# Attention and mixture of experts in one kernel: masks that read rows from partition 0, reversed keys for heads 4 to 7, and a later expert table

## The chip, the cores and the metric

The kernel runs on one core of a Trainium2 chip. The metric is the device time of one execution in microseconds (us). Five engines work beside each other, each through its own queue in order: PE (TensorE, matmuls and transposes), DVE (VectorE), ACT (ScalarE), POOL (GpSimd) and SP, which here only issues DMAs. POOL also issues the DMAs that scatter rows by an index. An engine's next instruction waits in its queue until the semaphores that it names have been raised, and what stands behind it waits too.

## The reference, cut to what matters

```python
# attention: q, k, v are (8, 8, 576, 64); ALiBi bias; a query sees itself and the 127 keys before it
scores = scale * (q @ k.T) + slopes[h] * -(pos_q - pos_k)
scores = where((rel >= 0) & (rel < 128), scores, -1e9)
attn = exp(scores - max); attn /= sum + 1e-9
x = (attn @ v) laid out as 4608 tokens of 512 values
# mixture of 8 experts, top 1
logits = (x / |x|) @ (expert_emb / |expert_emb|).T / tau
e = argmax(logits); gate = softmax(logits)[e]
out[token] = gate * (relu(x @ w1[e]) @ w2[e])
```

## The kernel before, in words

**Stages.** Attention comes first, up to about 243 us of the trace. The three large groups of tokens are routed to experts while it still runs, and the rows of each token are scattered to `xs`, a DRAM table sorted by expert. Then the largest expert's first 384 rows (the head) and all experts are multiplied. PE ends the program's chain in that second part.

**Tiles.** There are 36 attention tiles T: four pairs of batches times nine blocks of 64 queries (n = 0 to 8). A tile has two halves hf, of four heads each: hf 0 is heads 0 to 3, hf 1 heads 4 to 7. Partitions 0 to 63 of a score bank hold the queries of one batch, 64 to 127 those of the other. A half-tile takes this path: scores on PE into two PSUM banks (L588 adds the bias, L596 the products); with n > 1 a merge on DVE (L606) lays the far block of keys, of which only a triangle counts, into the masked triangle of the own block, so that 128 columns hold 192 keys; a maximum on DVE (L611); exponentials on ACT (L619); a transposition on PE (L627) after which keys lie on partitions; a copy to SBUF on ACT (L634, the tile `pq`); the mask on POOL (L647); the products with the values on PE (L658 for `pq`, L668 for the corners in `mb`); division on DVE (L682, L687); and the split of x into two fp16 parts (L703 on DVE, L714 on POOL), which L718 transposes by DMA for the logits (L724, L728).

**The mask.** After the transposition the 64 merged keys of a half-tile lie on partitions 0 to 63 or on 64 to 127: `mixed(T, hf)` is (n + hf) mod 2, and `halves[...]` picks that half of the partitions. Two POOL instructions of 64x512 take the merged block apart: the first writes one triangle to `mb`, the second leaves the other in `pq`. So of each tile's two masks one reads from partition 0 and one from partition 64: for even n it is hf 1 that reads from partition 64, for odd n hf 0. There are 56 masks, of 28 tiles with n > 1.

**Scatters.** `put` (L828, L829) issues one scattering DMA of a tile's 128 rows on POOL. Those of the first group of eight tiles stand among the masks of pair 1, those of the second among the masks of pair 2, and those of the third come in one row near attention's end.

**Order of the work.** The order on each engine is fixed at build time by a planner (`Plan`): each job has an engine, an estimated duration, what it comes after, the buffers that it takes, and a due time; the planner runs them in a model and emits them in that order. The planner's model has no wait of a mask for a scatter. PSUM has eight banks; `start` lets a job take a bank if its ring (`sc` 6 banks, `fl` 2, `ps` 4 for values, logits and the rest) has its oldest holder done, and if enough banks are open. The job `expert0` to `expert14` (L524 to L538) normalise the table of expert embeddings; `EXPERT` is the earliest planned time of them, in ns. The first of them, on DVE, needs the DMA of `tau`, which L492 issues behind two loads of keys, two of queries and the embeddings.

Of the kernel before, what the change touches and what calls it, by code (L numbers as in the profile page):

```python
# [23 lines left out]
P = 128  # L24
# [41 lines left out]
RING = {'sc': 'sc', 'fl': 'fl', 'av': 'ps', 'lg': 'ps', 'misc': 'ps'}  # L66
BANKS = {'sc': 6, 'fl': 2, 'ps': 4}
NBANK = 8
AHEAD = 4
ORDER = -1e9  # L70
KBUFS, QBUFS = 2, 4
VBUFS = 8
XBUFS = 16
# [6 lines left out]
SWITCH = 90  # L80
BOND = 5000
FREE = {"SP": 0, "POOL": 5300, "DVE": 4200, "PE": 3600, "ACT": 2100}
EXPERT = 6000
DUE = {'load': -13.7, 'loadv': -4.0, 'k': -7.0, 'q': -5.8, 'v': 2.0, 'score': 0.0, 'merge': 1.3, 'max': 2.0, 'exp': 3.5, 'flip': 3.8, 'phi': 3.3, 'mask': 5.6, 'av': 6.8, 'norm': 8.6, 'xhi': 7.1, 'xlo': 11.3, 'xnorm': 9.8, 'xdma': 10.5, 'logit': 9.6, 'route': 13.5, 'put': 16.7}


# [5 lines left out]
SHARE = {'x': 1, 'x2': 0.75}  # L92
QENG = ['ACT', 'DVE']
FENG = ['ACT']
PEBUFS, PQBUFS, MBUFS = 3, 4, 2


class Plan:
# [4 lines left out]
        self.yields = 0  # L103
        self.pooled, self.banks, self.given = (), [], []

    def job(self, name, eng, ns, emit, after=(), makes=(), uses=(), due=0.0, fill=False, early=0.0, dma=0, land=None, moves=0, port=False, lock=(), form=None):
        after = [a if isinstance(a, tuple) else (a, 0) for a in after]
        self.jobs[name] = dict(
            name=name, eng=eng, ns=ns, emit=emit, after=after, makes=list(makes), uses=list(uses), due=due, fill=fill, early=early, dma=dma, land=land, moves=moves, port=port, lock=lock, form=form
        )  # L110
# [18 lines left out]
    def run(self, free):  # L129
# [11 lines left out]
        def start(j):  # L141
            e = j["eng"]
            if "can" not in j:
                j["can"] = max([j["early"]] + [self.seen(a, j["name"], end) + extra for a, extra in j["after"]])
            t = max(free.get(e, 0.0), j["can"])
            seen = {}
            for ring, _ in j["makes"]:
                lst = rings.setdefault(ring, [])
                k = len(lst) + seen.get(ring, 0)
                seen[ring] = seen.get(ring, 0) + 1  # L150
                if k >= self.caps[ring]:
                    if k - self.caps[ring] >= len(lst):
                        return None
                    for u in self.users[lst[k - self.caps[ring]]]:
                        if u not in end:
                            return None
                        t = max(t, self.seen(u, j["name"], end))
            n = sum(1 for ring, _ in j["makes"] if ring in self.pooled)
            if n:
                open_ = sorted(opens(j))  # L160
                if len(open_) < n:
                    return None
                t = max(t, open_[n - 1][0])
            if j["port"]:
# [75 lines left out]
def kernel(  # L240
# [54 lines left out]
    nc.scalar.preload_act_table_set("natural_log_exp_and_others")  # L295
    ident = const.tile([P, P], F32, name="ident")
    make_identity(nc, ident)
    identb = const.tile([P, P], BF16, name="identb")
    nc.vector.tensor_copy(identb, ident)
    tab = const.tile([P, HP, 2 * P], BF16, name="tab")  # L300
# [21 lines left out]
    merges = [const.tile([P, 64], I32, name=f"merge_{i}") for i in range(2)]  # L322
# [24 lines left out]
    ones = const.tile([P, P], BF16, name="ones")  # L347
    nc.gpsimd.memset(ones, 1.0)
# [105 lines left out]
    def attention(actx):  # L454
# [114 lines left out]
        def mixed(T, hf):  # L569
            return (tiles[T][1] + hf) % 2  # L570
# [32 lines left out]
        def merge_dve(T, hf, j):  # L603
            ps, x = sc[T, hf, j], mixed(T, hf)
            lo, hi = ps[:, :, 0:64], ps[:, :, P : P + 64]
            nc.vector.copy_predicated(*((hi, lo) if x else (lo, hi))[:1], merges[x].unsqueeze(1).to_broadcast([P, 2, 64]), lo if x else hi)  # L606

        def max_dve(T, hf, j):
            nm_t[T, hf, j] = sm.tile([P, 2], F32, tag="nm", name=f"nm{j}_{T}_{hf}", bufs=8)
# [27 lines left out]
            return FENG[(2 * T + hf) % len(FENG)]  # L637

        def mask_pool(T, hf):
            n = tiles[T][1]  # L640
# [19 lines left out]
        def corners_pe(T):  # L660
            n = tiles[T][1]
            for i in range(4):
                for hf in range(2):
                    r = halves[mixed(T, hf)]
                    x = mb_t[T] if n else pq_t[T, hf]
# [314 lines left out]
        for T in range(NT):  # L980
# [22 lines left out]
            for hf in range(2):  # L1003
# [33 lines left out]
                if n > 1:  # L1037
                    ready = f"mask{u}"
                    J(
                        ready, "POOL", 1188, lock=(590, 590), emit=lambda a=a: mask_pool(*a), after=[f"phi{u}"], makes=[] if hf else [("mb", ("mb", T))],  # L1040
                        uses=[("pq", u), ("mb", T)], due=due("mask", u),
                    )
                J(
                    f"av{u}", "PE", 496 if n else 50, form="columns", emit=lambda a=a: values_pe(*a),
                    after=[ready] + then("put", T - XBUFS) + [f"v_one{x}" for x in vs], makes=[(RING["av"], ("av", u))],
                    uses=[("pq", u), ("av", u)] + [("v", y) for y in vs], due=due("av", u),
                )
            if n != 1:
                J(
                    f"avs{T}", "PE", 456, form="quarters", emit=lambda T=T: corners_pe(T), after=[f"av{u0}", f"av{u0 + 1}"],  # L1050
                    uses=[("av", u0), ("av", u0 + 1)] + ([("mb", T)] if n else [("pq", u0), ("pq", u0 + 1)]) + [("v", y) for y in vs], due=due("av", u0 + 1) + 300,
                )
            for hf in range(2):
                u = u0 + hf
                J(
                    f"recip{u}", "DVE", 95, lambda a=(T, hf): sums_dve(*a), after=[f"av{u}" if n == 1 else f"avs{T}"], makes=[("rs", ("rs", u))],
                    uses=[("av", u)], due=due("norm", u),
                )
                J(
                    f"norm{u}", "DVE", 332, lambda a=(T, hf): normalize(*a), after=[f"recip{u}"],  # L1060
                    makes=[] if hf else [("xf", ("xf", T))], uses=[("av", u), ("rs", u), ("xf", T)], due=due("norm", u) + 300,
                )
            u = u0 + 1
# [970 lines left out]
```

## Time and profile before

| | |
|---|---|
| median of 3 runs | 621.3 us (619.61 to 626.68) |
| the profiled execution | 624.13 us, of which the span from first to last instruction is 622.4 us |
| PE, DVE, ACT, POOL busy | 561.6, 459.8, 342.7, 259.9 us |
| mean granted clock of PE | 0.95 |
| first and last mask | 25.8 us, 239.3 us |
| first matmul of the experts behind the head (L1429) | 279.3 us |

Busy times are sums over stages with different limits; what a wait is worth is read from its own stage. A releaser in brackets is what ended an engine's idle time, by the profile's inference; of a wait for several semaphores it names the one that seems to have come last. Matmul ends are modelled.

### The profile page before, as it was taken

The numbers are of one execution on the slowest core, as the hardware profiler recorded it, in microseconds if no ns is written. First come the engines' busy times: TensorE is split into PE (matmuls) and PEld (weight loads), VectorE is DVE, ScalarE is ACT, GpSimd is POOL, SyncE is SP. The second block draws the span as 40 slices with busy tenths as digits, with TensorE's granted clock in tenths as the row PEclk, the third lists the DMA queues.
The fourth block names the chain that finished last, engine by engine and source line by source line (L and its number), as shares of the span: only waits on it lengthen the run. The fifth ranks groups of instructions, "written<-read, shape, count | busy, mean of one in ns | idle before, by whom it ended". The sixth has DMA issues, their size and how long they took to land.

```text
span 622.4 us, 17746 instructions
## 1 busy us (share of the span) xinstructions
PE 561.6 (90%) x6861; PEld 385.7 (62%) x6861; DVE 459.8 (74%) x1200; ACT 342.7 (55%) x804; POOL 259.9 (42%) x425
## 2 busy tenths in 40 slices
PE   5999978688589839989999999999999999999995
PEld 3778856477467726537565485475674764754885
DVE  3777983489349928826588698789899898789692
ACT  3877975477548824415255248348366374367541
POOL 4376557487557848450111403500503213104342
PEclk9999998799769955998999999999999999999999
DMA  8788985699859698569986927907929759525001
GB/s 286 168 180 219 240 212 148 160 225 210 235 115 198 105 275 166 171 181 311 198 256 129 336 73 190 309 31 177 325 60 279 206 100 332 119 62 159 31 2 70
DMA packets 135095, 112.81 MB, mean 181 GB/s; under 512 B 85589, under 2 KB 101461, under 8 KB 135008
## 3 DMA queue, kind: packets, MB, share of 16 engines
q1 hardware_dynamic: 124848, 85.39, 55.1%
q0 software_dynamic: 10160, 26.26, 14.9%
q8 instruction: 55, 0.90, 0.6%
q14 instruction: 32, 0.26, 0.1%
HBM read 73.08 MB, written 19.70 MB: 149 GB/s over the span
## 4 chain that ended last, share of the span: by engine, by line
PE 61%; POOL 13%; DMA 10%; DVE 10%; issue 4%; ACT 1%; SPq 1%; POOLq 0%; DVEq 0%; ACTq 0%
PE ps L1606 20%; DMA xs<-gx,di 7%; PE ps L1429 7%; PE ps7d L1449 5%; PE ps7c L1449 5%; PE ps7a L1449 5%; POOL pq L647 3%; POOL mb L647 3%; PE ps_head L909 3%; POOL xs L829 3%; POOL gx L714 3%; PE ps7b L1449 3%; PE av L658 2%; PE fl L627 2%; PE sc L596 2%
## 5 line engine op out<-in xcount | busy, mean ns | idle before, releaser
L447 POOL DMA_INDIRECT out_dram<-y,ids x32 | 49.5, 1546 | 218.7 <-ACT y L1618 151.8
L619 ACT ACTIVATE pe<-sc,nm 128x128 f32<-128x128 f32 x288 | 84.3, 384 | 14.3 <-DVE nm L611 12.2
L1606 PE MATMUL ps<-w2h,hh 128*128 128x512 f16 x224 | 84.9, 379 | 0.0
L1606 PE MATMUL ps<-w2h,hl 128*128 128x512 f16 x224 | 84.9, 379 | 0.0
L1606 PE MATMUL ps<-w2l,hh 128*128 128x512 f16 x224 | 84.9, 379 | 0.0
L1606 PEld LDWEIGHTS <-hh 128*128 128x128 f16 x448 | 43.7, 98 | 52.0 <-issue 0.8
L1449 PEld LDWEIGHTS <-w1h 128*128 128x128 f16 x672 | 65.7, 98 | 16.0 <-issue 1.4
L658 PE MATMUL av<-v,pq 128*64 128x65 f32 x1024 | 47.5, 242 | 29.1 <-POOL pq L647 27.4
L596 PE MATMUL sc<-k,ldq 64*64 64x192 f32 (+2 forms) x1216 | 59.6, 318 | 3.3 <-DVE ldq L553 2.7
L634 ACT COPY pq<-fl 128x512 f32<-128x512 f32 x72 | 41.6, 592 | 33.9 <-PE av L658 12.1
L658 PEld LDWEIGHTS av<-v,pq 128*64 128x64 f32 x1024 | 39.6, 152 | 31.1 <-POOL pq L647 29.4
L647 POOL TENSOR_SCALAR_AFFINE_SELECT mb<-pq 64x512 f32<-64x512 f32 x56 | 38.9, 694 | 44.9 <-DMA xs<-gx,di 24.5
L611 DVE TENSOR_REDUCE nm<-sc 128x2 f32<-128x256 f32 x144 | 55.5, 414 | 1.4 <-PE sc L596 1.3
L627 PE MATMUL fl<-ident,pe 128*128 128x128 f32 x288 | 49.4, 304 | 4.7 <-ACT pe L619 4.3
L714 POOL TENSOR_TENSOR gx<-xf,gx 128x512 f16<-128x512 f32 x36 | 41.8, 1162 | 22.8 <-DVE gx L703 20.3
L596 PEld LDWEIGHTS sc<-k,ldq 64*64 64x64 f32 x1216 | 43.3, 146 | 7.7 <-DVE ldq L553 3.1
L606 DVE COPY_PREDICATED sc<-merge,sc 128x128 f32<-128x128 int32 x112 | 29.0, 287 | 23.1 <-PE sc L596 15.0
L1429 PE MATMUL ps<-xT,w1h 128*128 128x288 f16 (+2 forms) x192 | 41.3, 310 | 2.6 <-DMA xT<-xs 2.6
L627 PEld LDWEIGHTS fl<-ident,pe 128*128 128x128 f32 x288 | 33.7, 151 | 13.8 <-ACT pe L619 9.9
L647 POOL TENSOR_SCALAR_AFFINE_SELECT pq<-pq 64x512 f32<-64x512 f32 x56 | 38.2, 681 | 3.9
L829 POOL DMA_INDIRECT xs<-gx,di x36 | 35.6, 990 | 8.1 <-issue 4.8
L1618 ACT ACTIVATE y<-ps,gs 128x512 f32<-128x512 f32 x24 | 16.3, 680 | 41.0 <-PE ps L1606 37.1
(286 smaller groups left out, 1384.8 us busy)
## 6 DMA issues: line engine op xcount, KB each, us to landing
ws<-moe_w_dram SPq DMA_DIRECT2D x46, 512.0 KB, 6.5
v<-v_dram SPq DMA_DIRECT2D x36, 260.0 KB, 4.9
ldq<-q_dram SPq DMA_DIRECT2D x36, 256.0 KB, 5.1
k<-k_dram SPq DMA_DIRECT2D x10, 768.0 KB, 5.8
ws_t<-moe_w_dram SPq DMA_DIRECT2D x12, 512.0 KB, 7.3
ws_t<-moe_w_dram POOLq DMA_DIRECT2D x12, 512.0 KB, 9.5
stg<-moe_w_dram SPq DMA_DIRECT2D x16, 256.0 KB, 3.1
ws_o<-moe_w_dram SPq DMA_DIRECT2D x3, 512.0 KB, 5.5
```

The costliest lines, as they stand in the source:

```text
L447: ins = nc.gpsimd.indirect_dma_start(out[:, :], bass.IndirectOffsetOnAxis(ap=ids, axis=0), y, None, bounds_check=NTOK - 1, oob_is_err=False)
L596: nc.tensor.matmul(sc[T, hf, j][o, l, c : c + w], qT[T][r, hp, o], kT[pr][r, a * HP + hp, at : at + w], start=False, stop=True, skip_group ...
L611: nc.vector.tensor_reduce(nm_t[T, hf, j], sc[T, hf, j][:, :, c : c + P], axis=AX.X, op=ALU.min)
L619: nc.scalar.activation(pr_t[T, hf][:, 2 * l + j, :], ps[:, l, c : c + P], AF.Exp, bias=nm[:, l : l + 1], scale=-1.0)
L627: nc.tensor.transpose(fl[:, i, :], pe[:, i, :], ident)
L647: nc.gpsimd.affine_select(y, i, pattern=[[0, 8], [sg, 64]], compare_op=ALU.is_ge if own else ALU.is_gt, fill=0.0, base=0, channel_multipli ...
L658: nc.tensor.matmul(px[o, i], pq_t[T, hf][:, i, o], vS[whole_v(T)[a]][:, 4 * hf + i], start=False, stop=n == 1, skip_group_check=True)
L714: nc.gpsimd.tensor_tensor(xx[:, DM : 2 * DM], xf_t[T], xx[:, 0:DM], op=ALU.subtract)
L829: ins = nc.gpsimd.indirect_dma_start(xs_rows[:, :], bass.IndirectOffsetOnAxis(ap=z["di"][:, g : g + 1], axis=0), X, None)
L1429: nc.tensor.matmul(ps[:, :w], a[:, kt, fs], xx[:, b + kt, c0 : c0 + w], start=(n == 0), stop=(n == len(jobs) - 1))
L1449: nc.tensor.matmul(ps, a[:, idx, c, fs], b[:, c, :], start=(n in OPENS and m == 0), stop=(m == len(jobs) - 1), skip_group_check=True)
L1606: nc.tensor.matmul(ps, x[:, ft, a * P : (a + 1) * P], w[:, ft, c], start=(n == 0), stop=(n == len(jobs) - 1))
```

## The change: what it does

- **Masks.** A mask whose merged keys lie on partitions 64 to 127 now reads and writes all 128 partitions, from partition 0; one with the keys on 0 to 63 stays at 64 partitions. So that partitions 0 to 63 pass unchanged in the instruction that works in place, the triangle's condition is laid from partition 0, and for heads 4 to 7 the 64 keys of each block stand in falling order: in `k` and `v` as the host lays them out, in the bias table (half of its columns are written from a reversed view), and in a second pair of merge masks. `mb` becomes a buffer per half-tile, four in all.
- **Expert table.** `EXPERT` goes from 6000 to 9500.
- **Planner.** PSUM's pooled rings no longer wait for the oldest holder; in its place `sc` and `fl` (`EARLY`) together take at most six of the eight banks and at most their own number, and the values of half 0 take a bank only where a second is open (`spare`). The division of half 1 comes after that of half 0.
- **Start.** The tile `ones` is set by DVE before the tables, not by POOL behind them.

```diff
-EXPERT = 6000
+EXPERT = 9500
+EARLY = ("sc", "fl", "ps1", "ps2")
-PEBUFS, PQBUFS, MBUFS = 3, 4, 2
+PEBUFS, PQBUFS, MBUFS = 3, 4, 4
...
+                if ring in self.pooled:
+                    continue
                 if k >= self.caps[ring]:
...
-                if len(open_) < n:
+                if len(open_) < n + j["spare"]:
                     return None
+                if j["makes"][0][1][0] in EARLY:
+                    free_ = {i for _, i in open_}
+                    busy = [key[0] for i, key in enumerate(self.banks) if i not in free_ and key[0] in EARLY]
+                    kind = j["makes"][0][0]
+                    if len(busy) + n > NBANK - 2 or sum(RING.get(x, "sc") == kind for x in busy) + n > BANKS[kind]:
+                        return None
...
-            nc.vector.tensor_scalar(tab[:, hp, c], rel[:, c], slopes[2 * hp], None, op0=ALU.mult)
+            i, o = (x.rearrange("p (b c) -> p b c", c=64) for x in (rel[:, c], tab[:, hp, c]))
+            nc.vector.tensor_scalar(o, i[:, :, ::-1] if hp >= HP // 2 else i, slopes[2 * hp], None, op0=ALU.mult)
...
-        for m, op in zip(merges, (ALU.is_ge, ALU.is_lt)):
-            nc.vector.tensor_scalar(m, near, 0.0, None, op0=op)
+        for hf in range(2):
+            for m, op in zip(merges[hf], (ALU.is_ge, ALU.is_lt)):
+                nc.vector.tensor_scalar(m, near[:, ::-1] if hf else near, 0.0, None, op0=op)
...
-            if T not in mb_t:
-                mb_t[T] = pp.tile([P, 4, P], F32, tag="mb", name=f"mb_{T}", bufs=MBUFS)
-            r = halves[mixed(T, hf)]
-            i, o = (x[r].rearrange("p h (a c) -> p (h a) c", c=64) for x in (pq_t[T, hf], mb_t[T]))
+            n, x = tiles[T][1], mixed(T, hf)
+            mb_t[T, hf] = pp.tile([P, 4, P], F32, tag="mb", name=f"mb_{T}_{hf}", bufs=MBUFS)
+            r = slice(0, 64 * (1 + x))
+            i, o = (y[r].rearrange("p h (a c) -> p (h a) c", c=64) for y in (pq_t[T, hf], mb_t[T, hf]))
+            step, base = (-1, 63 + 64 * x) if hf else (1, -64 * x)
             for y, own in ((o, n % 2 == 0), (i, n % 2 == 1)):
                 sg = 1 if own else -1
                 nc.gpsimd.affine_select(
-                    y, i, pattern=[[0, 8], [sg, 64]], compare_op=ALU.is_ge if own else ALU.is_gt, fill=0.0, base=0, channel_multiplier=-sg
+                    y, i, pattern=[[0, 8], [sg, 64]], compare_op=ALU.is_ge if own else ALU.is_gt, fill=0.0, base=-sg * base, channel_multiplier=-sg * step
                 )
...
-    values[..., odd, :] = np.roll(values[..., odd, :], 64, 3)
+    values[..., odd, :] = values[:, :, :, ::-1, odd]
```

## Rows read from the trace of the kernel before

**Rows 1.** The page's chain of waits: shares of the span by engine and line.

```profile
PE ps L1606 20%; DMA xs<-gx,di 7%; PE ps L1429 7%; PE ps7d L1449 5%; PE ps7c L1449 5%; PE ps7a L1449 5%; POOL pq L647 3%; POOL mb L647 3%; PE ps_head L909 3%; POOL xs L829 3%; POOL gx L714 3%; PE ps7b L1449 3%; PE av L658 2%; PE fl L627 2%; PE sc L596 2%
```

**Rows 2.** Timeline of POOL: start us, us, engine line op [idle before <-releaser].

```profile
25.84 0.73 POOL L647 TENSOR_SCALAR_AFFINE_SELECT mb<-pq 64x512 f32<-64x512 f32 x1 [3.99 <-ACT pq L634]
...
68.53 0.65 POOL L647 TENSOR_SCALAR_AFFINE_SELECT mb<-pq 64x512 f32<-64x512 f32 x1
...
155.16 0.96 POOL L829 DMA_INDIRECT xs<-gx,di  x1 [0.19 <-issue]
156.18 0.65 POOL L647 TENSOR_SCALAR_AFFINE_SELECT mb<-pq 64x512 f32<-64x512 f32 x1
...
157.53 1.15 POOL L714 TENSOR_TENSOR gx<-xf,gx 128x512 f16<-128x512 f32 x1
...
168.31 0.65 POOL L647 TENSOR_SCALAR_AFFINE_SELECT mb<-pq 64x512 f32<-64x512 f32 x1 [5.73 <-DMA xs<-gx,di]
...
230.04 1.13 POOL L647 TENSOR_SCALAR_AFFINE_SELECT mb<-pq 64x512 f32<-64x512 f32 x1 [7.56 <-ACT w1h L877]
```

**Rows 3.** Waits, whole run: engine line waited for: us in total, times, longest.

```profile
POOL mb L647 <- DMA xs<-gx,di: 24.5, 6, 5.7
...
DVE rtau L524 <- DMA rtau<-moe_tau_dram: 5.8, 1, 5.8
```

**Rows 4.** The chain of waits, in order of time: start us, us, what.

```profile
180.42 1.08 PE av L668 x32
...
186.33 0.64 PE av L668 x32
...
219.00 10.89 DMA xs<-gx,di
```

**Rows 5.** The scattering DMAs of line 829: time from issue to landing.

```profile
DMA to landing us min/median/max: 3.1/6.2/10.9
```

**Rows 6.** Stretches: length; PE, PEld, DVE, ACT, POOL busy (x instructions); clock, DMA, GB/s.

```profile
25.00:75.00 50.00, 47.66 (x1206) 39.01 (x1204) 40.32 (x143) 42.90 (x135) 34.84 (x52) 1.00 0.94 194
160.00:185.00 25.00, 15.08 (x276) 11.76 (x275) 8.12 (x28) 9.29 (x28) 13.69 (x23) 0.66 0.64 141
215.00:235.00 20.00, 8.03 (x122) 5.91 (x122) 7.72 (x26) 8.99 (x25) 11.22 (x18) 0.59 1.16 246
280.00:622.00 342.00, 333.97 (x2324) 213.88 (x2322) 274.02 (x504) 172.87 (x300) 82.48 (x81) 0.99 0.62 171
```

**Rows 7.** Timeline of PE, at the start and near attention's end.

```profile
10.83 1.13 PE L596 MATMUL sc<-k,ldq 64*64 64x128 f32 x16 [2.73 <-DVE ldq L553]
...
227.74 0.27 PE L724 MATMUL ptl<-enc,xT 128*128 128x16 f16 x4 [3.25 <-DMA xT<-gx]
...
231.94 1.14 PE L658 MATMUL av<-v,pq 128*64 128x65 f32 x16 [2.71 <-POOL pq L647]
```

**Rows 8.** The logits' matmuls: duration ns min/median/max, first and last start us.

```profile
L724 PE MATMUL ptl<-enc,xT x144: 169/169/194, 34.7 to 260.8; 128*128 128x16 f16 x144
```

**Rows 9.** Timeline of DVE: last instruction of the expert table.

```profile
17.21 0.19 DVE L538 SCALAR_TENSOR_TENSOR enc<-pt_en,enc 128x32 f16<-128x32 f32 x1 [1.17 <-ACT enc L537]
```

**Rows 10.** Groups on POOL, whole run: xcount, busy us, mean ns, idle before.

```profile
L309 POOL TENSOR_SCALAR_AFFINE_SELECT rel<-rel 64x64 f32<-64x64 f32 x2 | 0.5, 235 | 0.1
...
masks.py:199 POOL TENSOR_SCALAR_AFFINE_SELECT ident<-ident 128x128 f32<-128x128 f32 x1 | 0.3, 282 | 0.0
```

**Rows 11.** Groups on DVE in the first 20 us, columns as for POOL.

```profile
L330 DVE TENSOR_SCALAR merge<-near 128x64 int32<-128x64 f32 x2 | 0.3, 173 | 0.0
```

**Rows 12.** Timeline of one half-tile without a scatter in flight.

```profile
49.99 0.33 PE L588 MATMUL sc<-tab,identb 64*64 64x384 bf16 x4
...
52.13 1.68 ACT L619 ACTIVATE pe<-sc,nm 128x128 f32<-128x128 f32 x6
...
54.03 0.66 PE L627 MATMUL fl<-ident,pe 128*128 128x128 f32 x4
...
55.56 1.05 ACT L634 COPY pq<-fl 128x512 f32<-128x512 f32 x2
```

More of the change, by code (lines that the diff above doesn't have):

```diff
@@ L104, in __init__, with job @@
         self.pooled, self.banks, self.given = (), [], []
-    def job(self, name, eng, ns, emit, after=(), makes=(), uses=(), due=0.0, fill=False, early=0.0, dma=0, land=None, moves=0, port=False, lock=(), form=None):
+    def job(self, name, eng, ns, emit, after=(), makes=(), uses=(), due=0.0, fill=False, early=0.0, dma=0, land=None, moves=0, port=False, lock=(), form=None, spare=0):
         after = [a if isinstance(a, tuple) else (a, 0) for a in after]
         self.jobs[name] = dict(
-            name=name, eng=eng, ns=ns, emit=emit, after=after, makes=list(makes), uses=list(uses), due=due, fill=fill, early=early, dma=dma, land=land, moves=moves, port=port, lock=lock, form=form
+            name=name, eng=eng, ns=ns, emit=emit, after=after, makes=list(makes), uses=list(uses), due=due, fill=fill, early=early, dma=dma, land=land, moves=moves, port=port, lock=lock, form=form, spare=spare
         )
@@ L297 @@
     make_identity(nc, ident)
+    ones = const.tile([P, P], BF16, name="ones")
+    nc.vector.memset(ones, 1.0)
     identb = const.tile([P, P], BF16, name="identb")
@@ L321 @@
     near = const.tile([P, 64], F32, name="near")
-    merges = [const.tile([P, 64], I32, name=f"merge_{i}") for i in range(2)]
+    merges = [[const.tile([P, 64], I32, name=f"merge_{i}_{hf}") for i in range(2)] for hf in range(2)]
     def merge_rel():
@@ L346 @@
     tri = const.tile([P, P], BF16, name="tri")
-    ones = const.tile([P, P], BF16, name="ones")
-    nc.gpsimd.memset(ones, 1.0)
     nc.gpsimd.affine_select(
@@ L605, in merge_dve @@
             lo, hi = ps[:, :, 0:64], ps[:, :, P : P + 64]
-            nc.vector.copy_predicated(*((hi, lo) if x else (lo, hi))[:1], merges[x].unsqueeze(1).to_broadcast([P, 2, 64]), lo if x else hi)
+            nc.vector.copy_predicated(*((hi, lo) if x else (lo, hi))[:1], merges[hf][x].unsqueeze(1).to_broadcast([P, 2, 64]), lo if x else hi)
         def max_dve(T, hf, j):
@@ L639, in mask_pool @@
         def mask_pool(T, hf):
-            n = tiles[T][1]
-            if T not in mb_t:
-                mb_t[T] = pp.tile([P, 4, P], F32, tag="mb", name=f"mb_{T}", bufs=MBUFS)
-            r = halves[mixed(T, hf)]
-            i, o = (x[r].rearrange("p h (a c) -> p (h a) c", c=64) for x in (pq_t[T, hf], mb_t[T]))
+            n, x = tiles[T][1], mixed(T, hf)
[3 more added lines that the diff above has]
+            step, base = (-1, 63 + 64 * x) if hf else (1, -64 * x)
             for y, own in ((o, n % 2 == 0), (i, n % 2 == 1)):
@@ L664, in corners_pe @@
                     r = halves[mixed(T, hf)]
-                    x = mb_t[T] if n else pq_t[T, hf]
+                    x = mb_t[T, hf] if n else pq_t[T, hf]
                     for a, o in enumerate(halves):
@@ L1039, in attention @@
                     J(
-                        ready, "POOL", 1188, lock=(590, 590), emit=lambda a=a: mask_pool(*a), after=[f"phi{u}"], makes=[] if hf else [("mb", ("mb", T))],
-                        uses=[("pq", u), ("mb", T)], due=due("mask", u),
+                        ready, "POOL", 1188, lock=(590, 590), emit=lambda a=a: mask_pool(*a), after=[f"phi{u}"], makes=[("mb", ("mb", u))],
+                        uses=[("pq", u), ("mb", u)], due=due("mask", u),
                     )
@@ L1044, in attention @@
                     f"av{u}", "PE", 496 if n else 50, form="columns", emit=lambda a=a: values_pe(*a),
-                    after=[ready] + then("put", T - XBUFS) + [f"v_one{x}" for x in vs], makes=[(RING["av"], ("av", u))],
+                    after=[ready] + then("put", T - XBUFS) + [f"v_one{x}" for x in vs], makes=[(RING["av"], ("av", u))], spare=1 - hf,
                     uses=[("pq", u), ("av", u)] + [("v", y) for y in vs], due=due("av", u),
@@ L1050, in attention @@
                     f"avs{T}", "PE", 456, form="quarters", emit=lambda T=T: corners_pe(T), after=[f"av{u0}", f"av{u0 + 1}"],
-                    uses=[("av", u0), ("av", u0 + 1)] + ([("mb", T)] if n else [("pq", u0), ("pq", u0 + 1)]) + [("v", y) for y in vs], due=due("av", u0 + 1) + 300,
+                    uses=[("av", u0), ("av", u0 + 1)] + ([("mb", u0), ("mb", u0 + 1)] if n else [("pq", u0), ("pq", u0 + 1)]) + [("v", y) for y in vs], due=due("av", u0 + 1) + 300,
                 )
@@ L1059, in attention @@
                 J(
-                    f"norm{u}", "DVE", 332, lambda a=(T, hf): normalize(*a), after=[f"recip{u}"],
+                    f"norm{u}", "DVE", 332, lambda a=(T, hf): normalize(*a), after=[f"recip{u}"] + ([(f"norm{u0}", ORDER)] if hf else []),
                     makes=[] if hf else [("xf", ("xf", T))], uses=[("av", u), ("rs", u), ("xf", T)], due=due("norm", u) + 300,
@@ L2007 @@
     rows = np.pad(np.asarray(v).transpose(0, 2, 1, 3), ((0, 0),) * 3 + ((0, 1),))
+    keys = cols(k)
+    keys[:, :, :, H // 4 :] = keys[:, :, :, H // 4 :].reshape(B // 2, P, 2, H // 4, S // 64, 64)[..., ::-1].reshape(B // 2, P, 2, H // 4, S)
     n, odd = S // P * P, slice(H // 2, H)
     values = rows[:, :n].reshape(B // 2, 2, S // P, P, H, D + 1).transpose(0, 2, 1, 3, 4, 5).copy()
-    values[..., odd, :] = np.roll(values[..., odd, :], 64, 3)
+    values[..., odd, :] = values[:, :, :, ::-1, odd]
     last = rows[:, n:].reshape(B // 2, 2, 64, 2, H // 2, D + 1)
-    last = np.stack([last[:, :, :, 0], last[:, ::-1, :, 1]], 1).transpose(0, 1, 3, 2, 4, 5).reshape(B // 2, 1, P, H, D + 1)
+    last = np.stack([last[:, :, :, 0], last[:, ::-1, ::-1, 1]], 1).transpose(0, 1, 3, 2, 4, 5).reshape(B // 2, 1, P, H, D + 1)
     values = np.concatenate([values.reshape(B // 2, -1, P, H, D + 1), last], 1)
@@ L2015 @@
         "q": np.ascontiguousarray(blocks).reshape(-1, P, H * D),
-        "k": np.ascontiguousarray(cols(k)).reshape(B // 2, P, H, S),
+        "k": np.ascontiguousarray(keys).reshape(B // 2, P, H, S),
         "v": values.reshape(-1, P, H * (D + 1)),
```

## The prediction

> **What bounds the kernel now.** I read the page's chain of waits first. Most of it is PE work of the experts, which nothing here touches, but its second place, 7% of a span of 622.4 us or some 42 us, is a DMA, and not one that loads anything: the scatter of token rows into `xs` [rows 1]. A store on the path means that some instruction waits for it to land, so I went through POOL's timeline, scatters and masks alone. There a mask stands still after a scatter: 5.73 us before the one at 168.31, 7.56 us before the one at 230.04 [rows 2]. The list of waits gives six of the first kind, together 24.5 us; the seventh is put down to an ACT instruction [rows 2, 3], but in the chain the scatter issued at 219.00 lands 10.89 us later, at 229.89, and the mask starts 0.15 us behind that [rows 4], so I count it with the others. Together 32 us.
>
> **Which masks wait.** The tiles fall into the masks' order by count: 14 to a pair of batches, half 0 before half 1. All seven that wait are masks that read from partition 64. Seven masks that read from partition 0 begin within 3 us behind a scatter, while it is under way, and none of them waits: the one at 156.18 starts 0.06 us after POOL is done with issuing, and the `gx` subtraction at 157.53, which reads all 128 partitions from 0, doesn't wait either [rows 2]. A scatter lands 3.1 to 10.9 us after its issue, median 6.2 [rows 5]. So the wait belongs to the combination of "reads from partition 64" and "a scatter not yet landed". It sits in POOL's queue as a semaphore wait of its own; why it is there no row says.
>
> **What the waits do to the others.** With no scatter about, at 25 to 75 us, PE is busy 47.66 of 50 us. In the stretch with two waits it is 15.08 of 25 at a granted clock of 0.66, in the one with the long wait 8.03 of 20 at 0.59; DVE falls from 40 of 50 to 8 of 25 [rows 6]. Nothing else is full there, so these are stalls and not a full engine. The same 32 corner matmuls take 1.08 us behind a wait and 0.64 us a few microseconds later [rows 4]: PE at its lower level, 1.2 GHz, after idling, and back at 2.4. Behind 280 us PE is busy 334 of 342 us [rows 6], so what attention gains arrives at the end, since the experts start on the last rows scattered.
>
> **The change, part by part.**
>
> *The six waits* go, if a 128-partition read from partition 0 is treated as the `gx` one is: 24.5 us [rows 3]. What is late next is the mask's own input, ACT's copy; in the first case it was done 4.3 us before the mask began, when POOL fell idle, so I take the whole 24.5. Bounds: 12 (half of them find another wait) and 24.5.
>
> *The seventh wait* is worth less. Behind 219 us PE's queue is held by the logits, which wait 3.25 us for a transposing DMA until 227.74; only then come the value products, and PE's own wait for this mask is 2.71 us, to 231.94 [rows 7]. I take 2.7; bounds 0 and 7.6.
>
> *PE's lower clock* behind the waits: after the sixth the chain runs over PE from 180.42 to 186.33, 5.9 us, and its matmuls there are at 1.08 in place of 0.64 [rows 4], which costs at most 41% of it, 2.4 us; I take that. Behind the other waits I find POOL on the chain, and a slow PE beside it costs nothing. Bounds 0 and 8.4, if all of PE's busy time at lower clock counted in the two stretches (15.08 x 0.34 + 8.03 x 0.41) [rows 6].
>
> *The expert table.* DVE now stands 5.8 us before its first instruction, for the DMA of `tau` [rows 3]. Behind it wait the query scaling of tile 1, for which PE idles 2.73 us [rows 7], the rest of the tables and the maxima of tile 0. Moved 3.5 us back in the plan, behind these, it finds `tau` landed or nearly so, and what is then queued behind a rest of the wait is tile 1's and 2's DVE work. I take PE's 2.7; bounds 0 and 5.8. The table's ACT instructions and its PE transposition move with it; SP issues the same DMAs in the same order. Who needs the table are the logits, first at 34.7 us [rows 8]; it was ready at 17.4 [rows 9], so 17 us cover the shift, and without them the logits would hold PE's queue for what is over.
>
> *The masks themselves.* 28 of the 56 pairs of instructions go from 64 to 128 partitions. None in the trace has 128x512, but the same operation took 235 ns for 64x64 and 282 for 128x128 [rows 10]; from 64x64 to 64x512, at 0.65 us [rows 2], is 0.93 ns per column, which makes 295 for 64x128. Partitions cost nothing, columns do: 0. The far bound is a doubling, 56 instructions of 0.65 us or 36 us on POOL.
>
> *Setup.* Two more merge masks of 0.17 us on DVE [rows 11], in its queue between the maxima: -0.3. The reversed half of the bias table and `ones` on DVE fall into its wait for the tables and for `tau`: 0; without that cover, some 0.6. The four `mb` buffers hold as many tiles as two did: 0.
>
> *The bank rule* changes PE's order, and no row shows by how much. Scores and transpositions may hold six banks in place of eight; a half-tile without disturbance holds two score banks from 49.99 to 53.8 and one transposition bank from 54.03 to 56.6 [rows 12], so 2 x 3.8 + 2.6 = 10.2 bank-us, over six banks 1.7 us per half-tile. The pace of pair 0 is 68.53 - 25.84 = 42.7 us for 18 half-tiles [rows 2], 2.37 each: the limit does not bind. I take 0; bounds: 5 us of gain, and the loss in the third rival.
>
> **Sum**: 24.5 + 2.7 + 2.4 + 2.7 - 0.3 = 32.0 us. The profiled execution took 624.1 us (span 622.4 and 1.7 around it), which makes 592.1; the median of the runs shown is 2.8 us lower, so 589.
>
> **A rule beside a row.** How long a scatter is under way decides the term. The trace has 3.1 to 10.9 us, median 6.2 [rows 5]. The Trainium skill, "DMA: Bandwidth & Descriptors", section "Anatomy of one DMA — SWDGE (gpsimd) path", gives about 2.0 us plus the bytes at 436 GB/s; an estimate by that page for 128 rows of 2056 bytes is 2.6 us. By it each wait would be 3.6 us shorter, the six worth 3 us and the kernel after about 611. The rows contradict the page here: even the shortest landing is longer, and the DMA engines were shared with loads and transposes at the time.
>
> **Rivals.**
>
> *More than the waits comes back.* Everything runs at pair 0's pace: the 63 half-tiles between the masks at 25.84 and 230.04 [rows 2] at 2.37 us are 149.3 in place of 204.2, 54.9 saved and 2.7 at the start: 564. For it: PE is nearly full in pair 0 and nowhere so behind a wait. Against: pairs 1 to 3 have routing on DVE and 24 scatters of 1 us on POOL, which pair 0 lacks. 10%.
>
> *The wait moves to PE.* POOL no longer pauses, scatters follow each other more closely, and the transposing DMAs of `xT` land later; the logits stand in PE's queue in order, and all behind them waits, as at 227.74 [rows 7]. If each of the six waits turns into one of some 2.9 us, 17 of the 32 us are lost: 606. For it: the DMA engines were full at 215 to 235 (a share of 1.16). Against: at 160 to 185 the share is 0.64 [rows 6]. 15%.
>
> *Slower: the six banks bind.* If the banks' lives grow because routing holds DVE back, scores wait for banks, and PE for scores. The pace now is 204.2 us for 63 half-tiles, 3.24 with the waits in it. Six banks fall behind that from 19.4 bank-us per half-tile, 1.9 times the 10.2 [rows 12]; at 2.1 times, 21.4 bank-us, the pace is 3.57 and the 63 half-tiles take 20.8 us more, 2.7 of it back at the start: 639. For it: DVE is the engine with the most work per tile in the routing stretches. Against: the margin of 1.9. 5%.
>
> *The change doesn't do it.* A mask from partition 0 that reaches into partitions 64 to 127 still waits (against it stands the `gx` row at 157.53), which leaves the start's 2.7: 619; or the masks double and their 36 us eat the 30. 7%.
>
> **How the numbers follow.** My forecast has 63%; its own range is 573 (16 of the 19 us by which the upper bounds of the seventh wait, the clock, the start and the bank rule exceed the sum, 4.9 + 6.0 + 3.1 + 5) to 601 (the six waits at 12). The predicted time is 589. The range that is to hold 8 in 10 takes in the second rival and leaves out most of the first, the third and the fourth: 571 to 607. About 1%, or 6 us, is what a measurement of this kernel can tell from no change. Faster by more than that are the forecast and the first two rivals: 88%. Within it lies the fourth: 7%. Slower: 5%.
>
> **What would show it.** Right: no mask in the trace after waits for `xs`; a mask within 0.1 us of a scatter's issue wherever its `pq` is ready; the granted clock of PE at 1.00 from 25 to 200 us; L1429 starting some 32 us before 279. The start is right if the first mask comes near 23 us. The masks' price is right if the 128x512 form takes 0.65 to 0.7 us. The bank rule was free if the pace of pair 0 stays at 4.74 us per tile. Wrong: scatters that still end waits on POOL, PE waiting for `xT` in many places, or a pair 0 that is slower than before.

## The result, and the profile after

The changed kernel takes 588.37 us (median, 586.59 to 590.24) where the kernel before takes 620.45 beside it: a ratio of 0.9516, 95% interval 0.9435 to 0.9597. Timed again in the last set of experiments it took 588.89 us against 621.63, 0.9444 (0.9392 to 0.9495). Ratios are taken over the fast runs alone, so they are not the quotient of the medians. The forecast was 589, with a range of 571 to 607. The profiled execution took 590.24 us, of them 588.5 the span, against 624.1 and 622.4.

The page's chain of waits by line answers to [rows 1].

```profile
PE ps L1617 18%; PE ps L1440 7%; PE ps7d L1460 5%; PE ps7c L1460 5%; PE ps7a L1460 5%; PE sc L607 5%; PE fl L638 4%; PE av L669 3%; POOL xs L840 3%; PE ps7b L1460 3%; DMA ws<-moe_w_dram 2%; PE av L679 2%; PE ps_t L1607 2%; PE sc L599 2%; DMA stg<-moe_w_dram 2%
```

The second place, the scatters' landing with 7%, is gone from it; what is left of DMA are loads of weights. POOL's timeline shows it where it happened: a scatter (line 840 now) and the mask behind it (line 658). Columns as in [rows 2].

```profile
22.61 0.70 POOL L658 TENSOR_SCALAR_AFFINE_SELECT mb<-pq 64x512 f32<-64x512 f32 x1 [3.55 <-ACT pq L645]
...
83.29 0.97 POOL L840 DMA_INDIRECT xs<-gx,di  x1 [0.18 <-issue]
84.27 0.67 POOL L658 TENSOR_SCALAR_AFFINE_SELECT mb<-pq 128x512 f32<-128x512 f32 x1
...
147.21 0.97 POOL L840 DMA_INDIRECT xs<-gx,di  x1 [0.15 <-issue]
148.20 0.67 POOL L658 TENSOR_SCALAR_AFFINE_SELECT mb<-pq 128x512 f32<-128x512 f32 x1
```

In these two places a mask of 128 partitions starts 0.01 and 0.02 us after the scatter's issue is done, and no mask in the whole trace waits for a scatter. The landing itself is as slow as before: 3.0, 6.2 and 9.3 us at the least, the median and the most, beside [rows 5].

```profile
DMA to landing us min/median/max: 3.0/6.2/9.3
```

So the transfers have not become faster; nobody on POOL waits for them. The wider masks cost nothing in sum, as groups on POOL by form show (xcount, busy us, mean ns, idle before): 38.9 us for the 56 instructions of 128 partitions, 38.8 for the 56 of 64. The one that writes `mb` is a little shorter with 128 partitions, the one that works in place a little longer.

```profile
L658 POOL TENSOR_SCALAR_AFFINE_SELECT pq<-pq 128x512 f32<-128x512 f32 x28 | 20.1, 718 | 1.9
L658 POOL TENSOR_SCALAR_AFFINE_SELECT mb<-pq 64x512 f32<-64x512 f32 x28 | 19.8, 709 | 8.2 <-ACT pq L645 8.1
L658 POOL TENSOR_SCALAR_AFFINE_SELECT pq<-pq 64x512 f32<-64x512 f32 x28 | 19.0, 678 | 1.9
L658 POOL TENSOR_SCALAR_AFFINE_SELECT mb<-pq 128x512 f32<-128x512 f32 x28 | 18.8, 670 | 2.1 <-ACT pq L645 2.0
```

The stretches of [rows 6], by the same clock of the span:

```profile
25.00:75.00 50.00, 48.61 (x1226) 40.28 (x1224) 41.76 (x150) 43.16 (x135) 34.88 (x55) 1.00 0.93 204
160.00:185.00 25.00, 23.82 (x596) 19.01 (x589) 22.31 (x97) 19.43 (x60) 18.11 (x39) 1.00 0.90 174
215.00:235.00 20.00, 20.00 (x142) 11.13 (x140) 16.34 (x74) 7.78 (x19) 12.34 (x31) 1.00 0.68 219
```

PE is busy 23.8 of 25 us where it was 15.1, at a clock of 1.00 where it was 0.66. The first expert's first matmul, the start of the long stretch that nothing here touches, comes at 244.9 us, where it came at 279.3. The view of its line (duration ns, first and last start us):

```profile
L1440 PE MATMUL ps<-xT,w1h x192: 283/307/445, 244.9 to 296.4; 128*128 128x288 f16 x64, 128*128 128x352 f16 x64, 128*128 128x336 f16 x64
```

That is 34.4 us earlier, and the span is 33.9 us shorter: the whole gain lies ahead of the experts.

One sign of what follows is already in this trace. The list of PE's waits from 60 to 235 us had, before, 27.1 us for POOL's masks. Of those 0.3 are left, and a new releaser stands there that names no engine:

```profile
PE av L669 <- issue: 4.6, 3, 3.6
PE ptl L735 <- DMA xT<-gx: 3.8, 1, 3.8
...
PE sc L607 <- issue: 2.0, 2, 1.1
PE fl L638 <- issue: 1.7, 1, 1.7
```

"Issue" is time in which an engine waited for nothing that the profile shows. The kernel before has none of it on PE in this stretch; this one has 9.0 us over all lines. Two kinds of it will have to be told apart; what this kernel has is the second kind, of the last section.

### The profile page after: what moved, and what is told of

Its sections match the earlier page's. It is cut to its first block, busy times and chain, and to the rows that moved or that the text cites. A ratio compares the mean times of both kernels' runs of the same rounds, so it can differ in the third digit from the quotient of the medians.

```text
span 588.5 us, 17712 instructions
## 1 busy us (share of the span) xinstructions
PE 551.1 (94%) x6861; PEld 377.9 (64%) x6861; DVE 458.3 (78%) x1203; ACT 340.6 (58%) x804; POOL 259.4 (44%) x424
## 4 chain that ended last, share of the span: by engine, by line
PE 63%; DVE 14%; DMA 7%; POOL 7%; issue 4%; ACT 3%; SPq 1%; POOLq 0%; DVEq 0%; ACTq 0%
PE ps L1617 18%; PE ps L1440 7%; PE ps7d L1460 5%; PE ps7c L1460 5%; PE ps7a L1460 5%; PE sc L607 5%; PE fl L638 4%; PE av L669 3%; POOL xs L840 3%; PE ps7b L1460 3%; DMA ws<-moe_w_dram 2%; PE av L679 2%; PE ps_t L1607 2%; PE sc L599 2%; DMA stg<-moe_w_dram 2%
## 5 line engine op out<-in xcount | busy, mean ns | idle before, releaser
L669 PE MATMUL av<-v,pq 128*64 128x65 f32 x1024 | 44.6, 233 | 8.1 <-issue 4.6
L638 PE MATMUL fl<-ident,pe 128*128 128x128 f32 x288 | 46.5, 290 | 2.9 <-issue 1.7
L669 PEld LDWEIGHTS av<-v,pq 128*64 128x64 f32 x1024 | 37.4, 145 | 9.3 <-issue 5.0
L658 POOL TENSOR_SCALAR_AFFINE_SELECT mb<-pq 64x512 f32<-64x512 f32 (+1 forms) x56 | 38.6, 689 | 10.3 <-ACT pq L645 10.1
L658 POOL TENSOR_SCALAR_AFFINE_SELECT pq<-pq 64x512 f32<-64x512 f32 (+1 forms) x56 | 39.1, 698 | 3.8
L638 PEld LDWEIGHTS fl<-ident,pe 128*128 128x128 f32 x288 | 31.6, 144 | 12.1 <-ACT pe L630 4.5
L1617 PEld LDWEIGHTS <-hl 128*128 128x128 f16 x224 | 21.9, 98 | 26.5
```

Of the source, the lines that this page charges most:

```text
L638: nc.tensor.transpose(fl[:, i, :], pe[:, i, :], ident)
L658: nc.gpsimd.affine_select(y, i, pattern=[[0, 8], [sg, 64]], compare_op=ALU.is_ge if own else ALU.is_gt, fill=0.0, base=-sg * base, channel ...
L669: nc.tensor.matmul(px[o, i], pq_t[T, hf][:, i, o], vS[whole_v(T)[a]][:, 4 * hf + i], start=False, stop=n == 1, skip_group_check=True)
L1617: nc.tensor.matmul(ps, x[:, ft, a * P : (a + 1) * P], w[:, ft, c], start=(n == 0), stop=(n == len(jobs) - 1))
```

## The experiments

Twelve kernels in three sets, each set beside the kernel before on one chip. A per cent of it is some 6.2 us. The theory to start with was the prediction's own: the masks are worth some 30 us, the table 2.7, the rule on the banks nothing.

### The parts, one at a time

**masks_alone**: the masks from partition 0 with all that belongs to them (falling keys, four `mb` buffers, merge masks), the rest as before. Against the kernel after:

```
-EXPERT = 9500
+EXPERT = 6000
...
-                if ring in self.pooled:
-                    continue
...
-                if len(open_) < n + j["spare"]:
+                if len(open_) < n:
                     return None
-                if j["makes"][0][1][0] in EARLY:
...
```

(and `ones` and the order of the normalisations as before.)

> The kernel before with the masks' part alone (partition 0, reversed keys, a buffer mb per half-tile); the bank rule, EXPERT = 6000, the place of ones and the order of the divisions are those of before. If the waits for scatters are what counts (24.5 + 2.7 + 2.4 us by my terms), it takes 29 to 30 us less than before: 590 to 592, with no mask waiting for xs. If the planner's new order did most of it, the waits are gone here too but under half of the 32 us is: above 604. If the wait moves to PE, the trace shows PE waiting for xT where POOL no longer waits.

609.72 us, ratio 0.9759 (0.9717 to 0.9801). No mask waits for a scatter in its trace, and yet it gains 15 us, half of what was expected. By the number this is the sign of the rival ("under half of the 32 us"); the next run speaks against its reading that the planner's order did the rest by itself.

**all_but_masks**: the kernel after with the masks on partition 64 again, keys still falling.

```
-            r = slice(0, 64 * (1 + x))
+            r = halves[x]
...
-            step, base = (-1, 63 + 64 * x) if hf else (1, -64 * x)
+            step, base = (-1, 63) if hf else (1, 0)
```

> The changed kernel with its masks reading partitions 64 to 127 again where the merged keys lie there; reversed keys, bank rule, expert table and the rest stay. If the waits count, they are back, six to eight of them with 25 to 35 us of POOL's idle time, and only the start is gained: 615 to 618. If the planner's order did it: 600 or less.

617.63 us, 0.9856 (0.9808 to 0.9904). Its list of POOL's waits (us in total, times, longest):

```profile
POOL mb L658 <- DMA xs<-gx,di: 21.8, 5, 5.2
```

The time is in the range that was expected if the waits count; five waits are back where six to eight were expected. With two lines the waits are back: the partition at which the read starts decides whether the wait is there, and nothing else of the change does. Whether the chip asks for it or the program that was built puts it there, no run shows. Here the masks are worth 0.9856 against 0.9516 or 0.9444, 21 to 26 us.

**early_table**: the kernel after with `EXPERT = 6000`.

> The changed kernel with EXPERT = 6000. By my term the first mask comes 2.7 to 3.3 us later and the end too: 591 to 592. If attention takes up what the start loses (PE has idle time later on): under 1 us, 588 to 589.

613.44 us, 0.9828 (0.9789 to 0.9866): 19 to 24 us slower than the kernel after, for a table that moves the first mask from 22.6 to 26.1 us.

**old_banks**: the kernel after without the rule on the banks.

```
-                if ring in self.pooled:
-                    continue
...
```

> The changed kernel with the old bank rule (rings that wait for their oldest holder, no six-bank limit, no spare bank). By my term the rule is worth nothing: 587 to 590. If it was worth the 5 us that I allowed, 593; if the six banks bind, it is faster: 583 to 586.

602.99 us, 0.9647 (0.9609 to 0.9686): 8 to 13 us slower than the kernel after, for a rule that was costed at nothing.

**before_late_table** (`EXPERT = 9500` alone) and **before_banks** complete the set. The second is more than its expectation says: beside the rule it has the falling keys, the second pair of merge masks and the four `mb` buffers, with the masks on partition 64 and the table early.

> The kernel before with the expert table normalised late, and nothing else. By the terms of the prediction: 2.7 us less than before, some 622 us, its first mask near 22.6 us. Rival (the table's place is worth the 19 us that taking it out of the changed kernel cost): some 606 us.

614.46 us, 0.9883 (0.9842 to 0.9923): a gain of 7.3 us, neither the 2.7 of the terms nor the 17 of the rival.

> The kernel before with the rule on the banks of PSUM and nothing else. By the terms of the prediction: no change, 620 to 628 us. Rival (the rule is worth by itself the 9 us that taking it out of the changed kernel cost): some 616 us.

622.67 us, 0.9987 (0.9959 to 1.0015): no change, as by the terms.

All combinations, with PE's idle time on issue from 60 to 235 us, in brackets the part of it in waits that end 1.1 to 1.7 us after a packet of the instruction queue is done (the second kind), and the start of the 1st, 15th, 29th, 43rd and last mask. Two small parts of the change, `ones` on DVE and the order of the divisions, are in the rows with two or three crosses and not in the others; no run separates them.

| masks | table late | rule | ratio | issue, us | masks start at, us |
|---|---|---|---|---|---|
| | | | 1 | 0 | 25.8, 68.5, 131.3, 189.7, 238.3 |
| x | | | 0.9759 | 17.3 (6.1) | 26.7, 68.8, 122.5, 175.9, 222.5 |
| | x | | 0.9883 | 10.1 (0.2) | 21.7, 66.7, 125.1, 180.4, 227.0 |
| | | x | 0.9987 | 11.8 (4.1) | 26.0, 68.2, 130.1, 186.9, 232.8 |
| x | | x | 0.9828 | 14.3 (6.4) | 26.1, 68.5, 118.3, 176.9, 221.4 |
| x | x | | 0.9647 | 18.7 (9.4) | 22.2, 64.2, 118.3, 171.8, 216.7 |
| | x | x | 0.9856 | 8.4 (2.0) | 21.8, 63.6, 126.3, 181.7, 229.6 |
| x | x | x | 0.9516, 0.9444 | 9.0, 7.6 (all) | 22.6, 64.2, 117.6, 166.1, 206.5 |

Alone the three parts give 15.0, 7.3 and 0.8 us, 23.1 together; all at once they give 30 to 35. Masks and late table simply add up (0.9647). The rule, with the two small parts, costs 4 us beside the masks alone; by itself it gains 8 to 13 beside masks and table. A price that changes its sign with its company points to the order of the work and not to the banks themselves, though no run isolates that. The question became: what eats half of the masks' gain when they stand alone?

### What eats it: in part, runs of scatters

The chain of waits of masks_alone from 197 to 209 us (start us, us, what), with POOL issuing eight scatters in a row from 196.1 to 206:

```profile
197.21 0.52 PE av L661 x16
...
200.57 0.25 PE av L661
200.82 1.42 issue
202.24 0.22 PE av L661
202.46 0.54 issue
203.00 0.24 PE av L661
203.24 1.19 issue
204.43 0.26 PE av L671
204.69 1.15 issue
205.84 0.34 PE av L671
206.19 1.08 issue
207.26 0.35 PE av L671
...
207.97 1.07 PE av L671 x27
```

Sixteen matmuls that take 0.52 us at 197.21 are then started one at a time, up to 1.4 us apart, until 2 us after the last scatter was issued, and the rest follows at the lower clock, 1.2 GHz. Its stretches (columns as in [rows 6]):

```profile
190.00:200.00 10.00, 8.97 (x213) 7.03 (x201) 8.50 (x40) 6.67 (x20) 8.70 (x25) 1.00 0.39 91
200.00:210.00 10.00, 3.70 (x51) 2.87 (x55) 2.04 (x8) 2.48 (x9) 8.95 (x14) 0.65 1.11 282
210.00:220.00 10.00, 8.65 (x110) 6.53 (x106) 7.02 (x26) 6.94 (x19) 3.95 (x7) 0.67 0.73 188
```

POOL is nearly full with issuing, PE is busy 3.7 of 10 us, the clock falls to 0.65 and stays low for the next 10 us. The five other kernels with one cross or two show the same at their run of eight, with 3.0 (all_but_masks) to 8.1 us (before_late_table) of idle time on issue beside the 7.4 here, and less of it, 1.6 to 3.4 us, at a run of five to seven between 137 and 163 us. The kernel before and the kernel after have a run of eight too, and no such wait. The sum in the table is a sign and no price: before_banks has 11.8 us of it, waits 16 us less for masks, and takes as long as the kernel before.

**masks_spread**: masks_alone with the scatters of the first three groups kept apart. **after_spread**: the same in the kernel after.

```
-after=[done, f"mark{T0 + g}", f"xlo{T0 + g}"]
+after=[done, f"mark{T0 + g}", f"xlo{T0 + g}"] + ([(f"put{T0 + g - 1}", 1300)] if g and gi <= GP else [])
```

> The kernel before with the change to the masks alone, and with each scatter of the first three groups let start no sooner than 1.3 us after the end of the one ahead of it in its group, so that masks stand between them in POOL's queue. Theory (the masks' gain is partly eaten by runs of five to eight scatters, in which the matmuls start one by one with idle time put down to issue, 17 us between 60 and 235 us, and by the half clock behind them): the idle time on issue falls under 6 us and the time goes from 609.7 us to 592 to 598 us. Rival A (the planner's order as a whole, POOL too full): the idle time on issue may fall, the time stays within 4 us of 610 us. Rival B (the later scatters make the next stage late): 612 us or more.

604.19 us, 0.9700 (0.9662 to 0.9739), 0.6% or 3.7 us better than masks_alone by the ratios, just clear of noise, where 12 to 18 were expected. By the number that is Rival A, which allowed 4 us. The theory's own sign came out all the same: idle time on issue falls from 17.3 to 3.3 us, and the last mask comes at 205.8 us, 16.7 earlier. But the span shrinks by 9.0 only, because another wait has taken over at the end of attention. (Of the 3.3 us 2.3 are of the second kind; of the first, 1.0 is left of 11.2.) The list of PE's waits from 195 to 245 us, and the place in PE's timeline:

```profile
PE ptr L773 <- DVE oh L810: 12.7, 2, 8.1
```

```profile
211.12 0.24 PE L731 MATMUL ptl<-enc,xT 128*128 128x8 f16 x4
219.49 0.18 PE L773 MATMUL ptr<-oh,tri 128*128 128x32 bf16 x1 [8.13 <-DVE oh L810]
...
219.62 0.80 PE L912 MATMUL ps_head<-x_head,w1h 128*128 128x384 f16 x2
```

The ranking matmul of the next group stands in PE's queue ahead of the first expert's block (`ps_head`), and DVE, which has split that expert's weights meanwhile, is 8.1 us late with its input. Attention was faster, and what is behind it was not. The rival that named the later scatters as the cause was right on the place and wrong on the culprit: the wait is for DVE.

> The kernel after with the same spacing of the scatters of the first three groups. Theory: there is little on issue to win here (9 us between 60 and 235 us, most of it outside the runs of scatters), so 588 to 594 us beside some 594 us for the kernel after on this scale; the last of the eight scatters ahead of the head block come some 10 us later, which may cost up to 5 us. Rival A (order alone): anything from 590 to 605 us. Rival B: the head block waits for the later scatters and the time is 600 us or more.

604.89 us, 0.9690 (0.9648 to 0.9733): 11 to 15 us slower than the kernel after. The theory's 588 to 594 us failed; the time is at the upper end of what Rival A allowed, and over the 600 of Rival B, whose head block waiting for the scatters is not in PE's list. Its idle time on issue stays at 9.6 us, 8.9 of it of the second kind, and PE waits 6.4 us for the same `oh`. The kernel after has no wait of the first kind that spreading could remove, so here it only disturbs.

**after_again** is the kernel after, for a narrower interval.

> The kernel after, unchanged, beside the others of this set: some 594 us where the kernel before takes 623 to 625 us (ratio 0.952), with a narrower interval than its first runs gave.

588.89 us, 0.9444 (0.9392 to 0.9495).

**two_groups_spread** and **third_in_pairs**: masks and late table without the rule (old_banks), with the first two groups spread; the third group in one run, or in pairs.

```
+ ([(f"put{T0 + g - 1}", 1300)] if g and gi < GP else [])
```

```
+ ([(f"put{T0 + g - 1}", 1300 if gi < GP else 1300 * (g % 2 == 0))] if g and gi <= GP else [])
```

> The masks and the late expert table without the rule on the banks (603 us), with the scatters of the first two groups spaced by 1.3 us and the eight of the third left in one run. Theory (runs of scatters starve PE): no idle time on issue near the scatters of the first two groups, 3 to 7 us of it in the third run near 190 to 200 us; the last mask moves from 216.7 to 207 to 211 us and the head block, which needs only the third run, is not late: 594 to 598 us. Rival (order alone): within 3 us of 603 us.

595.45 us, 0.9566 (0.9526 to 0.9606). The last mask comes at 208.3 us, as expected, but the detail was wrong: the third group's eight scatters, in one run from 175.1 to 185.4 us, leave no idle time on issue on PE, and the 5.3 us that it has lie ahead of 160 us, in single pauses of at most 2.2. All of it is of the second kind. A run of eight does not always hold PE back.

> As the kernel with two groups spaced, and the third group's eight scatters in pairs with a mask or more between the pairs. Theory: the idle time on issue in the third run falls under 2 us and the last mask comes near 203 to 206 us; the last scatter comes 4 to 5 us later than in one run, and the head block starts some 17 us behind it, at 212 to 216 us: 594 to 600 us, no better than with two groups. If the head block is not late: 588 to 592 us, faster than the kernel after. Rival (order alone): within 3 us of 603 us.

590.00 us, 0.9515 (0.9464 to 0.9566), with the last mask at 204.6 us, 4.3 us of idle time on issue, and the head block at 208.55, not late. The spread scatters gain 8 us over old_banks' 0.9647, about what the rule on the banks gains there; the kernel is as fast as the kernel after was at first (0.9516), and beside its 0.9444 in this set the intervals overlap. No version beat the kernel after.

Its last stretches show what stands next in the way:

```profile
180.00:190.00 10.00, 6.70 (x130) 4.97 (x130) 8.37 (x25) 7.69 (x21) 9.41 (x12) 1.00 1.09 260
190.00:200.00 10.00, 6.04 (x161) 4.98 (x162) 8.35 (x20) 8.06 (x19) 9.73 (x13) 1.00 1.24 258
```

```profile
PE av L661 <- POOL pq L650: 5.6, 6, 1.8
```

POOL itself is full, 9.4 and 9.7 of 10 us, and PE waits for its masks again, 5.6 us from 195 to 245 us: no mask waits for a scatter here, and POOL has next to no idle time left.

**after_8000**: the kernel after with `EXPERT = 8000`.

> The kernel after with the expert table let start at 8.0 instead of 9.5 us of the plan, between its two values tried so far. By the term for the table (its place at the start is all that counts): 594 to 598 us with the first mask between 22.6 and 26.1 us. By the theory that the order it gives to later work decides (where the runs of scatters fall): anything between 594 and 613 us, with the difference to the kernel after made behind 60 us, and more idle time on issue than the 9 us of the kernel after where it is slow.

591.23 us, 0.9519 (0.9473 to 0.9565), first mask at 21.7 us. It is close to the kernel after, not to early_table, and its first mask is as early as with 9.5: the 19 us lie between 6.0 and 8.0 us of the plan, and the order at 9.5 is no single lucky point. Of the 19 some 4 are there at the first mask; between the 29th and the 43rd early_table takes 58.6 us and this kernel 45.9, and in that stretch early_table has its run of seven scatters and a clock of 0.54 from 150 to 160 us. A run of seven stands in this kernel too, from 137.5 to 146.1 us, and no wait on issue beside it.

## Why the prediction was right, point by point

The total was right, and so was the mechanism for the masks. The terms were not: two of them were too small and one too large, and that they made up for each other to within a microsecond is luck.

*Which masks wait, and that a read from partition 0 does not*: right. all_but_masks brings the waits back with two lines.

*The six waits (24.5), the seventh (2.7) and the clock (2.4)*: together 29.6 were forecast. By themselves the masks give 15 us, within the bound of 12 that I had put and then not used ("half of them find another wait"). The step that failed is "what is late next is the mask's own input ... so I take the whole 24.5". The copies were early enough, for all six by 7 us and more. What came next was on PE: its own starts were late, 17.3 us of issue, 10.6 of it beside the runs of scatters, and its clock was low behind them; spreading the scatters took the issue to 3.3 us and the last mask 16.7 us ahead, and PE then waited for DVE's ranking. A part of the gain turned into new waits, one after the other. Beside the late table the masks are worth 15 us too (before_late_table to old_banks), beside the rule 10 (before_banks to early_table); only in the order that table and rule make together are they worth 21 to 26 us.

*The expert table (2.7)*: too small, and its bound of 5.8 too. The first mask comes 3.5 to 4.6 us earlier with it, a little more than PE's wait [rows 7], and alone it gives 7.3 us. That is not the start's gain carried to the end: in before_late_table the first mask is 4.2 us ahead, the 15th only 1.8, the last 11.3. Most of it is made behind the 15th mask, where scatters and masks meet in another order; which meeting pays it, no run isolates.

*The bank rule (0, at best -5)*: right alone (0.8 us, within the interval of no change), and outside the bounds beside the others, 8 to 13 us. The step that failed was to cost it by its limit on banks and not by what it does to the order. It was in the text ("changes PE's order, and no row shows by how much"), and the bound of 5 was too narrow for that.

*Masks of 128 partitions (0), merge masks (-0.3)*: right for the first, 670 and 718 ns beside 709 and 678; the second is too small to be seen.

*The Trainium skill's rule on a scatter's time*: the trace after has 3.0, 6.2 and 9.3 us to landing, and all_but_masks waits 21.8 us in five places. The Trainium skill, "DMA: Bandwidth & Descriptors", section "Anatomy of one DMA — SWDGE (gpsimd) path", from which 2.6 us was estimated, would have led to about 611 us; the measurement decides against it. But it is not the shortest landing that contradicts this figure, as the prediction says. The rows count from the start of POOL's issuing instruction, of some 1.0 us, and know the landing of 16 scatters of 36 (22 in the kernel after); from that instruction's end the shortest takes 2.2 us (1.9) and the median 5.2, in both kernels.

*The rivals.* PE waits for `xT` once, 3.8 us, not in many places. Attention did not run at pair 0's pace throughout: from the first to the last mask the kernel after takes 183.9 us, 28.5 less than the kernel before, where that rival had 54.9 less up to the seventh wait. The six banks did not bind: in PE's list from 60 to 235 us no score waits for another engine. The masks neither wait nor double.

*What would show it*: the experts' start came 34.4 us earlier (32 forecast) and the first mask at 22.6 us (23). The pace of pair 0 is 41.5 us, 1.2 shorter than before, so the rule did no harm there. The clock was not at 1.00 from 25 to 200 us: it is 0.83 from 110 to 120 and 0.74 from 190 to 200.

## What to carry to other kernels

The time of a wait is not what its removal gives: the masks, forecast at 29.6 us, gave 15 alone, and the table, at 2.7 and at most 5.8, gave 7.3. Look which queue behind a wait is next to its limit, here POOL's issuing, PE's starts and DVE's ranking, and put the lower bound where two of them take back their share. A change that passes through a planner's order has no price of its own: time each part alone and all together before its terms are trusted, and widen the range by the spread between orders: taking one part out of the whole change cost 8 to 13 us (the rule) or 19 to 24 (the table). And read the row whose releaser names no engine: "issue" was the line in the list of masks_alone that pointed to where a part of the gain had gone. But look where each of its waits stands before adding them up: two kinds share the name.

## What the runs showed of the hardware that was not expected

*PE can be held back while POOL issues scatters in a row.* In masks_alone 10.6 of the 17.3 us of issue lie between the first scatter of a run (five from 142.2 us, eight from 196.1) and 2 us behind its last; matmuls that wait for nothing the trace shows start one by one, often some 0.7 or 1.4 us apart. Putting masks between the scatters takes the sum to 3.3 us. It does not happen in every run of eight: six kernels have it there, and five have not, among them the kernel before (210 to 220 us), the kernel after (183 to 193) and two_groups_spread (175 to 185). What decides it is open; no run here separates the bytes in flight from the issuing itself.

*A second kind of issue wait ends 1.2 to 1.6 us after a packet of instructions is done,* with or without a scatter near. In the kernel after PE stands 3.65 us until 115.43, in the middle of sixteen matmuls:

```profile
111.24 0.54 PE L669 MATMUL av<-v,pq 128*64 128x65 f32 x11
115.43 0.39 PE L669 MATMUL av<-v,pq 128*64 128x65 f32 x5 [3.65 <-issue]
```

The DMA queues of 113 to 114 us show the one packet of the instruction queue between 112 and 117 us, and the page its count over the span (packets, MB, share):

```profile
q8 instruction: 1, 0.02, 5.8%
```

```profile
q8 instruction: 54, 0.88, 0.6%
```

In masks_alone a wait of 2.36 us until 120.39 likewise follows the packet of 118 to 119 us. The Trainium skill, "Runtime: NRT & Kernel Launch", section "Instruction fetch mechanics", says that instructions are fetched in blocks of 16 KiB and that crossing into the next one is mostly hidden. The size agrees (0.88 MB in 54 packets); hidden it is not always, as these two waits suggest.

The traces say more than these two. In the kernel after, its repetition, after_8000, two_groups_spread and third_in_pairs there are 30 waits of PE on issue from 60 to 235 us, and every one ends 1.2 to 1.6 us after such a packet is done. Each of these kernels has 26 packets in that stretch, so the stretches from 1.2 to 1.6 us behind a packet are 10 of 175 us, some 6% of the time, which rules out chance; 19 to 21 of the 26 packets pass without a wait. The kernel before has 24 packets there and no such wait. That the packet was late, and not something else that goes with it, was not tried: no run moved a packet.
